# Loading, casting and transposing the first two batches in another way in a sparse attention and MLP kernel

## The chip, the cores and the metric

The kernel runs on one core of a Trainium2 chip. The metric is the device time of one execution in microseconds, the median of several runs. A core has the engines PE (TensorE: matmuls and transposes), DVE (VectorE), ACT (ScalarE), POOL (GpSimd) and SP (SyncE, which here only issues transfers). They run side by side, each in its own fixed order, and wait for one another through semaphores. Transfers run on 16 DMA engines. In this kernel SP and ACT issue theirs to one kind of queue (hardware_dynamic in the profile) and POOL to another (software_dynamic), and only transfers that POOL issues change the type on the way.

## What is computed

```python
B, H, S, D = 8, 8, 576, 64            # batches, heads, tokens, head size; 8 global tokens
scores = q @ k^T / sqrt(D)            # per batch and head
mask = (|i - j| <= 32) | is_global[i] | is_global[j]
attn = softmax(where(mask, scores, -1e9))
x = (attn @ v) laid out as [B * S, H * D]            # 4608 x 512
h = x @ w_in                                         # 512 x 2048
out = (relu(h) ** 2) @ w_out                         # 2048 x 512
```

All inputs come as fp32, the token indices as int64, and the output is fp32. Inside, the kernel works in fp16 with fp32 accumulation.

## The kernel before

**Unit of work.** Attention is done for one pair of heads of one batch at a time: pair i is heads 2(i mod 4) and the next one of batch i // 4, so i = 0 to 3 is batch 0 and i = 4 to 7 is batch 1. A pair has two halves of the query columns. For each half, `sc_mm` makes the scores in PSUM, `sc_exp` takes the exponential on ACT, `pv_mm` multiplies by the values and by a block of ones (for the row sums), `pv_rec` makes reciprocals on ACT with a logarithm and an exponential, and `pv_mul` on DVE writes the result into `xT` (or `xA`, for half 0 of batch 0).

**Masking.** It is done in one of two ways. Where `added(i, half)` is true, PE first adds a large negative number to the masked places, with a matmul of an identity and the tile `far` ahead of the scores. Elsewhere `sc_mask` on DVE multiplies the exponentials (tile `er`) by 0 or 1 (into tile `et`).

**Keys and queries.** Batches 0 and 1 are loaded as token rows by `fetch_tokens`, 96 partitions of 6 tokens for each head. Pairs 0 and 1 come as fp32 into `stf`. Pairs 2 and 3 (into `s16a`, a part of `mix`) and 4 to 7 (into `s16b`) come through POOL's queue, and turn to fp16 on the way. `cast_tokens` then copies each pair to a tile `natk` or `natq`, with the two heads side by side; for the fp16 rows this copy only changes the layout. `transpose` puts these tiles through PE, six token groups at a time, and adds a product with a one-hot matrix that picks the global tokens. `place_k` and `place_q` copy the result to `kt` and `qt`. A switch, `wide`, decides whether a weight of 128 columns is used whole or in two halves of 64; it is off in batch 0 and on in batch 1.

**Values.** `fetch_values` brings a pair's values into the fp32 tile `stv` (a part of `early`) from SP's queue, one DMA for each of 5 tiles of 120 tokens. `cast_values` makes the fp16 tile `vts[i]` from it. In batch 0 this runs on DVE (pairs 0 and 3), POOL (pair 1) and ACT (pair 2). `values_sum` and `values_place` then gather the global tokens' values and put them in rows 0 to 7 of each tile.

**Batches 2 to 7** take another way: fp16 copies in DRAM (`kscr`, `qscr`), transposed by DMA (`fetch_transposed`, SP), and values cast by DMA.

**Global query tokens.** Their columns are set afterwards by `scatter` on POOL, a copy for each token to a column whose number stands in a POOL register. `load_columns` reads those eight registers.

**The MLP** is cut into parts (`mm1`, `mm1_half`, `mm2`, `mm2_fast`) that stand in a list, `fills`. `fill` and `take` put them between the attention steps. `w_in` and `w_out` come through POOL's queue in four DMAs each.

**Order.** Nothing is scheduled automatically: each engine runs its instructions in the order of the program's text. The order of batch 0 is written out by hand (L888 to L1016), batch 1 has a loop (L1032 to L1055). `keep_warm` and `warm` are matmuls without use that fill waiting time on PE. Before SP brings batch 1's values, a small DMA named `gate` (L1012) reads a piece of `w_in`, so SP stands there until that piece has landed.

Of the kernel before, what the change touches and what calls it, by code (L numbers as in the profile page):

```python
# [17 lines left out]
KT = 120  # L18
NT = 5
KN = (120, 120, 120, 120, 96)  # L20
# [30 lines left out]
def kernel(  # L51
# [57 lines left out]

    def token_rows(nm, i):  # L110
        x = "kq".index(nm)
        if i < 2:
            one = stf[0:TP, x, 2 * FW * i : 2 * FW * (i + 1)]
        elif i < NHP:
            one = s16a[0:TP, x, 2 * FW * (i - 2) : 2 * FW * (i - 1)]
        else:
            one = s16b[0:TP, x, 2 * FW * (i - NHP) : 2 * FW * (i - NHP + 1)]
        return one.rearrange("p (h f) -> p h f", h=2)

# [29 lines left out]

    def fetch_tokens(eng, nm, i):  # L150
        b, hp = divmod(i, NHP)
        eng.dma_start(
            out=token_rows(nm, i),
            in_=src[nm][b, 2 * hp : 2 * hp + 2].rearrange("h (p j) d -> p h (j d)", j=TJ),
        )

    def fetch_values(eng, b, hp):
        hs = slice(2 * hp, 2 * hp + 2)
        for t in range(NT):
            r0 = 0 if t and not b else 8  # L160
            eng.dma_start(
                out=stv[r0 : 8 + KN[t], t, hs],
                in_=v[b, hs, KT * t + r0 - 8 : KT * t + KN[t]].rearrange("h s d -> s h d"),
            )

    kscr, qscr = {}, {}
# [52 lines left out]
    fetch_values(nc.sync, 0, 1)  # L219
    for hp in range(2, NHP):  # L220
        fetch_values(nc.sync, 0, hp)

# [4 lines left out]
    nc.vector.memset(onesb, 1.0)  # L227
    nc.vector.memset(stv[0:NG, 0], 0.0)
    pidx = sbt("pidx", [P, 4], I32)
# [56 lines left out]
    for i in range(2, NHP):  # L286
        fetch_tokens(nc.gpsimd, "k", i)
        fetch_tokens(nc.gpsimd, "q", i)


    wide = [False]

    def column_tiles():
        return (slice(0, P),) if wide[0] else (slice(0, D), slice(D, P))
# [190 lines left out]
    def transpose(nm, i, idles=0):  # L485

        nat = nats[(nm, i)]
        tr = pst("mm", [P, 1024], FP16)
        warm(tr.bitcast(FP32), idles)
        for j in range(TJ):  # L490
            for r in column_tiles():
                nc.tensor.transpose(
                    tr[r, TP * j : TP * j + TP], nat[:, j, r], identity[0:TP, 0:TP]
                )
        gl = tr.bitcast(FP32)[:, 384 : 384 + NG]
        for j in range(TJ):
            halves(
                gl, nat[:, j, :], ohp[0:TP, j, :], start=(j == 0), stop=(j == TJ - 1),
                skip_group_check=True,
            )  # L500
        trs[(nm, i)] = tr[:, 0:S].rearrange("p (j q) -> p q j", j=TJ), gl
# [250 lines left out]
    def added(i, half):  # L752
        return i < NHP and (half == 0 or i < 2) or NHP <= i < 2 * NHP and half == 0

# [134 lines left out]
    keep_warm(4)  # L889
    load_columns()  # L890
    index_base()
# [26 lines left out]
    mask_globals(mg, 1)  # L918
    cast_values(pool.tensor_copy, 1)
    casts0(2)  # L920
    sc_mm(1, 0, 2)
# [11 lines left out]
    pv_mul(0, 0)  # L933
    casts0(3)
    values_sum(1)
# [6 lines left out]
    place_q(3)  # L942
    cast_values(act, 2)
    pv_mm(1, 0)
    pv_mm(0, 1)
    cast_values(vec, 3)
    values_sum(2)
# [24 lines left out]
    for i in range(4):  # L972
        pool.dma_start(out=w_in[:, :, ts(i, 512)], in_=wv[:, :, ts(i, 512)])
    def tokens1(i):
        for nm in "kq":
            cast_tokens(vec, nm, i)

    def transposes1(i):
# [4 lines left out]

    for i in range(NHP, 2 * NHP - 1):
        fetch_tokens(pool, "k", i)
        fetch_tokens(pool, "q", i)
    scatter(0, slice(0, NHP - 1), xA)
# [10 lines left out]
    pv(2, 1)  # L998
    pv(3, 1)
    scatter(0, slice(NHP - 1, NHP), xA)  # L1000
    fetch_tokens(pool, "k", 2 * NHP - 1)
    fetch_tokens(pool, "q", 2 * NHP - 1)
    nc.scalar.copy(out=xT[:, :, 256:HS], in_=xA[:, :, 256:HS])
    for u in range(0, 8, 2):
        fills.pop(0)
        mm1_half(u, 0, range(NDM - 1, NDM))
    tokens1(NHP)
    for j in range(4):
        pool.dma_start(out=w_out[:, ts(j, 4), :], in_=wo[:, ts(j, 4), :])
    scatter(0)  # L1010
    gate = dram.tile([1, 8], FP16, name="gate")
    nc.sync.dma_start(out=gate, in_=w_in[0:1, 0, 3 * 512 : 3 * 512 + 8])  # L1012
    nc.sync.dma_start(
# [9 lines left out]
    transposes1(NHP)  # L1023
    tokens1(NHP + 1)
    take(2)
# [6 lines left out]
    for i in range(NHP, 2 * NHP):  # L1032
        scores(i, 0)
        fill(1)
        if prev is not None:
            pv(*prev)
        if i + 1 < 2 * NHP:
            transposes1(i + 1)
        fill(1)
        scores(i, 1)  # L1040
        pv(i, 0)
        if i + 2 < 2 * NHP:
            tokens1(i + 2)
        if i + 1 < 2 * NHP:
            values1(i + 1)
        fill(2)
        prev = (i, 1)
        if i == NHP:
            open_batch(2)
            fetch_batch_globals(2)  # L1050
        elif i == NHP + 1:
            fetch_batch(2, "k")
        elif i == NHP + 2:
            fetch_batch(2, "q")
            fetch_batch_values(2)  # L1055
# [75 lines left out]
```

## Time and profile before

| | |
|---|---|
| median of 5 runs | 327.25 us (327.0 to 327.77) |
| the profiled execution | 326.49 us |
| its span, first to last instruction | 324.7 us |
| PE busy / DVE / ACT / POOL | 310.3 / 244.7 / 202.2 / 127.8 us |
| mean granted TensorE clock | 0.992 |
| DMA packets, data | 149919, 39.32 MB |

The profile is of one execution. All its times are microseconds from the start of the span. A row of the timeline has the start, the length, the engine, the line of the kernel, the operation, output<-input, the shape and a count, and in brackets the idle time of that engine just before with what ended it. A line such as L298 is that of a helper that all matmuls of a kind share, so the names of the tiles tell them apart. PEld is PE loading weights, which goes on beside its matmuls. A busy PE is not PE at its peak, and the ends of matmuls are modelled.

### The profile page before, as it was taken

To read this page: it belongs to the slowest core of one execution; us is meant where nothing else is said; L and a number is where in the kernel's file an instruction comes from. 1 tells how busy PE (TensorE), PEld (TensorE's weight loads), DVE (VectorE), ACT (ScalarE), POOL (GpSimd) and SP (SyncE) were. 2 spreads that over 40 slices of the span, in tenths; PEclk is the share of its full clock that TensorE was granted. 3 is DMA by queue.
4 is the path that set the end of the run, shared out by engine and by line. 5 is a ranking of instruction groups with operands and counts; after the bars stand their busy time and mean duration, and the time that the engine had idled before them with its cause. 6 is when DMAs were issued, how large, how long until landed. Compare 5 with 4: busy or idle time off the path is not lost.

```text
span 324.7 us, 11457 instructions
## 1 busy us (share of the span) xinstructions
PE 310.3 (96%) x4739; PEld 234.9 (72%) x4739; DVE 244.7 (75%) x601; ACT 202.2 (62%) x380; POOL 127.8 (39%) x222
## 2 busy tenths in 40 slices
PE   7887899999999999999999999999999999999995
PEld 4655677445588758975999856985698569868995
DVE  6774599558997788678867869876987698768465
ACT  3684687536856685768547487658765876373150
POOL 8558697348801950289001970059302000100000
PEclk9998999999999999999999999999999999999999
DMA  8999999989995999599923699559996301200211
GB/s 193 181 193 206 191 193 167 152 108 203 138 116 77 193 163 99 77 187 142 135 94 87 53 176 152 73 108 189 136 99 129 97 0 35 100 1 2 85 48 67
DMA packets 149919, 39.32 MB, mean 121 GB/s; under 512 B 133124, under 2 KB 149300, under 8 KB 149868
## 3 DMA queue, kind: packets, MB, share of 16 engines
q0 software_dynamic: 95408, 16.78, 65.6%
q1 hardware_dynamic: 54042, 21.23, 34.8%
q8 instruction: 37, 0.61, 0.8%
q10 hardware_dynamic: 418, 0.59, 0.7%
q14 instruction: 14, 0.11, 0.1%
HBM read 37.86 MB, written 17.29 MB: 170 GB/s over the span
## 4 chain that ended last, share of the span: by engine, by line
issue 45%; POOL 22%; PE 12%; DMA 9%; POOLq 1%; ACT 1%; DVE 0%
PE mm L298 12%; DMA qscr<-in_q_dram 6%; POOL kscr L178 6%; POOL xT L873 5%; POOL s16b L207 3%; DMA kscr<-in_k_dram 3%; POOL qscr L185 3%; POOL stf L207 1%; POOL gstq L435 1%; POOL gstk L435 1%; POOL gstv L435 1%; POOLq L873 1%; ACT rec L822 0%; ACT rec L821 0%; ACT rl L543 0%
## 5 line engine op out<-in xcount | busy, mean ns | idle before, releaser
L298 PE MATMUL mm<-xT,w_in 128*64 128x512 f16 (+2 forms) x1216 | 122.5, 351 | 0.2 <-POOL xT L873 0.2
L298 PEld LDWEIGHTS <-w_in 128*64 128x64 f16 (+1 forms) x1280 | 80.1, 109 | 45.6 <-issue 3.4
L543 ACT ACTIVATE rl<-mm 128x512 f16<-128x512 f32 x128 | 75.0, 598 | 36.1 <-PE mm L298 34.3
L545 DVE TENSOR_TENSOR gt<-rl 128x512 f16<-128x512 f16 x128 | 53.0, 423 | 23.0 <-ACT rl L543 21.9
L298 PEld LDWEIGHTS <-mix 128*64 128x64 f16 x1280 | 68.8, 110 | 1.7
L873 POOL COPY xT<-gx 128x4 f16 x64 | 18.0, 282 | 130.5 <-DVE xT L852 127.1
L779 ACT ACTIVATE er<-at 128x880 f16<-128x880 f32 x54 | 46.1, 904 | 14.5 <-PE at L770 13.0
L630 DVE TENSOR_TENSOR mix<-gt 128x1024 f16<-128x1024 f16 (+1 forms) x82 | 52.9, 673 | 0.2
L789 DVE TENSOR_TENSOR et<-er,mask 128x880 f16<-128x880 f16 x54 | 33.2, 617 | 16.8 <-ACT er L779 16.2
L298 PE MATMUL mm<-early,mix 128*64 128x256 f16 x768 | 45.4, 273 | 0.0
L821 ACT ACTIVATE rec<-at 128x288 f32<-128x288 f32 x64 | 25.8, 404 | 27.1 <-PE at L811 21.9
L298 PEld LDWEIGHTS <-gt 128*64 128x64 f16 (+1 forms) x596 | 33.1, 109 | 9.8 <-DVE gt L545 2.2
L852 DVE TENSOR_TENSOR xT<-at,rec 128x288 f16<-128x288 f32 x60 | 27.2, 454 | 9.3 <-ACT rec L822 8.9
L298 PE MATMUL mm<-early,gt 128*64 128x256 f16 x512 | 32.2, 274 | 1.0 <-DVE gt L545 1.0
L298 PE MATMUL mm<-w_out,mix 128*64 128x256 f16 x512 | 30.9, 273 | 0.0
L811 PE MATMUL at<-et,onesb 128*64 128x192 f16 (+5 forms) x400 | 29.8, 225 | 0.0
L822 ACT ACTIVATE rec<-rec 128x288 f32<-128x288 f32 x64 | 28.4, 443 | 2.0
L665 DVE TENSOR_TENSOR ot<-mm,pt 128x512 f32<-128x512 f32 (+1 forms) x36 | 22.7, 632 | 6.5 <-ACT pt L690 5.2
L178 POOL DMA_DIRECT2D kscr<-in_k_dram x30 | 26.6, 1076 | 1.2 <-DMA w_out<-in_moe_w_out_dram 0.9
L185 POOL DMA_DIRECT2D qscr<-in_q_dram x24 | 23.8, 1397 | 0.5 <-DMA gscr_k<-gstk 0.5
L690 ACT COPY pt<-mm 128x512 f32<-128x512 f32 (+1 forms) x18 | 9.7, 540 | 20.6 <-PE mm L298 20.6
L811 PEld LDWEIGHTS <-onesb 128*64 128x64 f16 x400 | 21.8, 110 | 0.7
(119 smaller groups left out, 327.3 us busy)
## 6 DMA issues: line engine op xcount, KB each, us to landing
out_dram<-ot SPq DMA_DIRECT2D x32, 256.0 KB
qscr<-in_q_dram POOLq DMA_DIRECT2D x24, 144.0 KB, 8.9
kscr<-in_k_dram POOLq DMA_DIRECT2D x24, 120.0 KB, 6.0
w_in<-in_moe_w_in_dram POOLq DMA_DIRECT2D x4, 512.0 KB, 9.2
w_out<-in_moe_w_out_dram POOLq DMA_DIRECT2D x4, 512.0 KB, 12.1
stf<-in_v_dram POOLq DMA_DIRECT2D x12, 120.0 KB, 10.3
s16b<-in_v_dram POOLq DMA_DIRECT2D x12, 120.0 KB, 8.2
early<-in_v_dram SPq DMA_DIRECT2D x20, 60.0 KB
```

The source lines that it names most:

```text
L178: nc.gpsimd.dma_start(out=kscr[b][r0 : r0 + KN[t]].rearrange("s (h d) -> s h d", d=D), in_=k[b, :, KT * t : KT * t + KN[t]].rearrange("h s ...
L185: nc.gpsimd.dma_start(out=qscr[b][r0 : r0 + GTOK].rearrange("s (h d) -> s h d", d=D), in_=q[b, :, GTOK * g : GTOK * (g + 1)].rearrange("h ...
L298: nc.tensor.matmul(to[r], weights[:, r], moving, **flags)
L543: nc.scalar.activation(out=rl, in_=ph, func=AF.Relu)
L545: nc.vector.tensor_tensor(out=gt[:, :, 0:T], in0=rl, in1=rl, op=ALU.mult)
L630: nc.vector.tensor_tensor(out=gsums[p][:, lo:hi, 0:TH], in0=g[0], in1=g[1], op=op)
L779: nc.scalar.activation(out=er[:, :, 0:W], in_=scs.pop((i, half))[:, :, 0:W], func=AF.Exp, bias=0.0, scale=scale)
L789: nc.vector.tensor_tensor(out=et[:, :, 0:W], in0=er[:, :, 0:W], in1=mask[:, MB[half] : MB[half] + W].unsqueeze(1).to_broadcast((P, 2, W)), ...
L811: nc.tensor.matmul(acc[D * e : D * e + D, x, o : o + w], onesb if x else vt[:, t, e], et[:, e, so : so + w], start=(n == 0), stop=(n == le ...
L822: nc.scalar.activation(out=rec, in_=rec, func=AF.Exp, scale=-1.0)
L852: nc.vector.tensor_tensor(out=(xT if x0 else xA)[:, hp, x0 : x0 + HS].rearrange("p (k x) -> p k x", k=2), in0=av[:, 0, :, 0:GTOK], in1=rec ...
L873: nc.gpsimd.tensor_copy(out=xb[:, :, ds(gv[g], 1)], in_=gxs[b][:, pairs, g : g + 1])
```

## The change

The change has these parts:

- Values of pairs 0 and 1 still come as fp32 by SP, in three DMAs a pair instead of five. Those of pairs 2 and 3 are loaded by POOL straight into `vts[2]` and `vts[3]`, cast on the way, behind the token rows of pairs 2 and 3 and ahead of the gather and of `w_in`. Their casts on ACT and DVE are gone. Pair 1's cast moves from POOL to DVE.
- No value DMA writes rows 0 to 7 in batch 0 any more, so these are cleared first, on DVE.
- Token rows that are already fp16 (pairs 2 to 7) are transposed from where the DMA put them. `cast_tokens` is used for pairs 0 and 1 alone, and transposes and one-hot products always work in two halves of 64.
- Batch 1's pairs 5 to 7 come with one DMA for k and one for q.
- `load_columns` stands behind batch 1's loads instead of at the program's start.
- Two of the four `w_out` DMAs go ahead of the last pair's `scatter`; the gate reads chunk 2 of `w_in` instead of chunk 3.
- `added` is no longer true for half 0 of batch 1, so these scores are masked on DVE.

```diff
-    def token_rows(nm, i):
+    def token_rows(nm, i, n=1):
...
-            one = s16b[0:TP, x, 2 * FW * (i - NHP) : 2 * FW * (i - NHP + 1)]
-        return one.rearrange("p (h f) -> p h f", h=2)
+            one = s16b[0:TP, x, 2 * FW * (i - NHP) : 2 * FW * (i - NHP + n)]
+        return one.rearrange("p (h f) -> p h f", f=FW)
...
-    def fetch_values(eng, b, hp):
+    def fetch_values(eng, b, hp, to=None):
         hs = slice(2 * hp, 2 * hp + 2)
-        for t in range(NT):
-            r0 = 0 if t and not b else 8
+        to = stv[:, :, hs] if to is None else to
+        n = NT - 1
+        for h in range(2):
             eng.dma_start(
-                out=stv[r0 : 8 + KN[t], t, hs],
-                in_=v[b, hs, KT * t + r0 - 8 : KT * t + KN[t]].rearrange("h s d -> s h d"),
+                out=to[8 : 8 + KT, 0:n, h],
+                in_=v[b, 2 * hp + h, 0 : KT * n].rearrange("(t s) d -> s t d", s=KT),
             )
+        eng.dma_start(
+            out=to[8 : 8 + KN[n], n],
+            in_=v[b, hs, KT * n : S].rearrange("h s d -> s h d"),
+        )
...
-    for hp in range(2, NHP):
-        fetch_values(nc.sync, 0, hp)
...
-    nc.vector.memset(stv[0:NG, 0], 0.0)
+    nc.vector.memset(stv[0:NG, :, 0 : 2 * 2], 0.0)
+    for vt in vts[2:NHP]:
+        nc.vector.memset(vt[0:NG], 0.0)
...
     for i in range(2, NHP):
         fetch_tokens(nc.gpsimd, "k", i)
         fetch_tokens(nc.gpsimd, "q", i)
+    for i in range(2, NHP):
+        fetch_values(nc.gpsimd, 0, i, vts[i])
...
     def transpose(nm, i, idles=0):
-        nat = nats[(nm, i)]
+        if i < 2:
+            nat = nats[(nm, i)].rearrange("p j (h d) -> p j h d", d=D)
+        else:
+            nat = token_rows(nm, i).rearrange("p h (j d) -> p j h d", d=D)
...
-            for r in column_tiles():
+            for h, r in enumerate((slice(0, D), slice(D, P))):
                 nc.tensor.transpose(
-                    tr[r, TP * j : TP * j + TP], nat[:, j, r], identity[0:TP, 0:TP]
+                    tr[r, TP * j : TP * j + TP], nat[:, j, h], identity[0:TP, 0:TP]
                 )
...
-            halves(
-                gl, nat[:, j, :], ohp[0:TP, j, :], start=(j == 0), stop=(j == TJ - 1),
-                skip_group_check=True,
-            )
+            for h, r in enumerate((slice(0, D), slice(D, P))):
+                nc.tensor.matmul(
+                    gl[r], nat[:, j, h], ohp[0:TP, j, :], start=(j == 0), stop=(j == TJ - 1),
+                    skip_group_check=True,
+                )
...
     def added(i, half):
-        return i < NHP and (half == 0 or i < 2) or NHP <= i < 2 * NHP and half == 0
+        return i < NHP and (half == 0 or i < 2)
...
     keep_warm(4)
-    load_columns()
     index_base()
...
-    cast_values(pool.tensor_copy, 1)
-    casts0(2)
+    cast_values(vec, 1)
...
-    casts0(3)
...
-    cast_values(act, 2)
...
-    cast_values(vec, 3)
...
-    for i in range(NHP, 2 * NHP - 1):
-        fetch_tokens(pool, "k", i)
-        fetch_tokens(pool, "q", i)
+    for nm in "kq":
+        fetch_tokens(pool, nm, NHP)
+    for nm in "kq":
+        fetch_tokens(pool, nm, NHP + 1, NHP - 1)
+    load_columns()
     scatter(0, slice(0, NHP - 1), xA)
...
     pv(3, 1)
+    for j in range(2):
+        pool.dma_start(out=w_out[:, ts(j, 4), :], in_=wo[:, ts(j, 4), :])
     scatter(0, slice(NHP - 1, NHP), xA)
-    fetch_tokens(pool, "k", 2 * NHP - 1)
-    fetch_tokens(pool, "q", 2 * NHP - 1)
...
-    tokens1(NHP)
-    for j in range(4):
+    for j in range(2, 4):
         pool.dma_start(out=w_out[:, ts(j, 4), :], in_=wo[:, ts(j, 4), :])
...
-    nc.sync.dma_start(out=gate, in_=w_in[0:1, 0, 3 * 512 : 3 * 512 + 8])
+    nc.sync.dma_start(out=gate, in_=w_in[0:1, 0, 2 * 512 : 2 * 512 + 8])
...
-    tokens1(NHP + 1)
...
-        if i + 2 < 2 * NHP:
-            tokens1(i + 2)
```

More of the change, by code (lines that the diff above doesn't have):

```diff
@@ L148, with fetch_tokens @@
     gscr = {}
-    def fetch_tokens(eng, nm, i):
+    def fetch_tokens(eng, nm, i, n=1):
         b, hp = divmod(i, NHP)
         eng.dma_start(
-            out=token_rows(nm, i),
-            in_=src[nm][b, 2 * hp : 2 * hp + 2].rearrange("h (p j) d -> p h (j d)", j=TJ),
+            out=token_rows(nm, i, n),
+            in_=src[nm][b, 2 * hp : 2 * (hp + n)].rearrange("h (p j) d -> p h (j d)", j=TJ),
         )
-    def fetch_values(eng, b, hp):
+    def fetch_values(eng, b, hp, to=None):
         hs = slice(2 * hp, 2 * hp + 2)
-        for t in range(NT):
-            r0 = 0 if t and not b else 8
+        to = stv[:, :, hs] if to is None else to
+        n = NT - 1
+        for h in range(2):
             eng.dma_start(
-                out=stv[r0 : 8 + KN[t], t, hs],
-                in_=v[b, hs, KT * t + r0 - 8 : KT * t + KN[t]].rearrange("h s d -> s h d"),
-            )
+                out=to[8 : 8 + KT, 0:n, h],
+                in_=v[b, 2 * hp + h, 0 : KT * n].rearrange("(t s) d -> s t d", s=KT),
+            )
+        eng.dma_start(
+            out=to[8 : 8 + KN[n], n],
+            in_=v[b, hs, KT * n : S].rearrange("h s d -> s h d"),
+        )
     kscr, qscr = {}, {}
@@ L973 @@
         pool.dma_start(out=w_in[:, :, ts(i, 512)], in_=wv[:, :, ts(i, 512)])
-    def tokens1(i):
-        for nm in "kq":
-            cast_tokens(vec, nm, i)
     def transposes1(i):
```

## The prediction

> **What bounds the kernel now.** I read the page first, then busy time by stretch, then the timeline of the first 65 us engine by engine, then the DMA view of single stretches.
>
> The page and the busy time by stretch (columns: stretch, its length, then busy us and count for PE, PEld, DVE, ACT, POOL; granted TensorE clock, DMA share, GB/s):
> ```profile
> PE 310.3 (96%) x4739; PEld 234.9 (72%) x4739; DVE 244.7 (75%) x601; ACT 202.2 (62%) x380; POOL 127.8 (39%) x222
> ...
> 20.00:30.00 10.00, 6.24 (x107) 4.24 (x107) 6.37 (x21) 7.53 (x16) 5.04 (x19) 0.98 1.26 204
> 30.00:40.00 10.00, 8.59 (x95) 6.66 (x94) 4.36 (x11) 4.83 (x11) 7.27 (x15) 0.85 1.26 197
> 40.00:50.00 10.00, 10.00 (x140) 7.80 (x138) 8.77 (x29) 8.07 (x16) 8.45 (x9) 1.00 1.32 194
> ```
> From 40 us on PE is full: what takes PE work away there is worth its own time, and what only relieves DVE or POOL is worth nothing. Before about 39 us PE waits in chains with the other engines, and there one late step moves everything behind it, to the end. So I ask two things: how far does the start of the w_in product (28.96) move, and how much PE work between 36 and 65 us goes or comes.
>
> DVE in the opening (start, length, engine and line, what):
> ```profile
> 0.93 0.27 DVE L224 MEMSET idle<- 128x256 uint32 x1 [0.93 <-PEq L1115]
> ...
> 1.46 0.48 DVE L228 MEMSET early<- 8x512 f32 x1
> ...
> 2.03 0.19 DVE L309 MEMSET oh<- 128x160 uint32 x1
> ...
> 5.45 0.20 DVE L328 TENSOR_TENSOR ohp<-gbf,tokp 128x48 f16<-128x48 f32 x1
> 5.57 0.55 DVE L455 CAST natk<-stf 96x768 f16<-96x768 f32 x1
> 7.33 0.66 DVE L506 COPY kt<-mm 128x480 f16<-128x480 f16 x1 [1.21 <-PE mm L298]
> ```
> DVE runs without a gap from 0.93 to the cast of the first k rows; those landed at 3.8 by the trace's landing records. PE transposes them at once. DVE is therefore the opening's critical engine.
>
> DVE late in batch 0, and below it PE from there into batch 1:
> ```profile
> 22.09 0.23 DVE L463 CAST early<-early 104x128 f16<-104x128 f32 x1 [1.40 <-DMA early<-in_v_dram]
> 22.23 0.47 DVE L478 COPY early<-gvs 8x640 f16<-8x640 f16 x1
> ```
> ```profile
> 23.92 0.56 PE L298 MATMUL at<-far,identity 128*64 128x440 f16 x4 [0.49 <-DVE mix L852]
> ...
> 28.96 4.45 PE L298 MATMUL mm<-mix,w_in 128*128 128x256 f16 x24 [1.49 <-ACT er L779]
> ...
> 38.59 0.43 PE L492 MATMUL mm<-identity,natk 96*128 96x96 f16 x6 [0.29 <-DVE natk L455]
> ...
> 41.16 0.54 PE L298 MATMUL at<-far,identity 128*128 128x440 f16 x2
> ...
> 41.63 0.36 PE L770 MATMUL at<-qt,kt 64*128 64x160 f16 x6
> ```
> On DVE, the engine stands 1.40 us for the last tile of pair 3's values, with pairs 2 and 3's placing queued behind it. That tile left SP at 15.1 and landed at 22.1, beside w_in packets.
>
> **The change part by part.**
>
> *Opening memsets.* L228 grows from 512 to 1280 f32 elements per row. 512 took 0.44 to the next start, 0.86 ns each, so 1280 take 1.10: +0.66. Two memsets of 640 fp16 are added. If written as 320 words, like idle (256 words, 0.24 to the next start), 0.29 each; if as fp16 elements, at the 0.12 us per 128 of the ones memset (1.17 to 1.29), 0.6 each. I take the words, as idle, oh and kt are fp16 tiles that the trace shows as uint32: +0.58. Together +1.2, at most +1.9. Nothing covers it: the mask copies, one_hots, natk at 5.57, PE's transposes at 6.17 and place_k at 7.33 follow on DVE or wait for it. ACT's q cast (6.26 to 7.09) has its own start, but q's transposes stand behind k's on PE. From 13.86 to 19.75 PE is unbroken by its own order, fillers included, so the delay is carried to there: **+1.2**.
>
> *Casts out of batch 0.* On DVE pairs 2 and 3's token casts go (0.34+0.34, 0.56+0.34), pair 1's value cast comes over from POOL (0.98 there, 0.55 on DVE as for pair 0). The token casts lie before or beside that unbroken PE stretch: nothing gained; if PE were not full there, at most 0.7. Pair 1's value cast waits for its values. They were in at 13.3 with SP held back for free slots; now SP issues six DMAs at once, and DVE comes to the cast at about 14: no wait, and 0.5 us of slack before place_k(2).
>
> *Later values.* ACT's cast (0.82 at 19.26) and DVE's (with its wait) go. Without the opening's shift: values_sum(2) starts at 19.75 instead of 19.93 and runs through in 0.4; scores(3,0) end at 21.1, not 21.48; exp 21.15 to 22.08; pv_mm(2,0) at 22.2, not 22.75, ending 22.9. On DVE placing of pair 2 is at 20.6, of pair 3 at 21.6 to 22.35, pv_mul(1,0) ends at 22.75, so PE's scores(1,1) start at 22.9, not 23.92, and end at 23.75. ACT has the reciprocals of (2,0) done at 23.83, so its exp starts at 23.85 instead of 24.82: **-0.95**. The rest up to 28.96 hangs on that exp. ACT's own order stops a larger gain.
>
> *POOL's queue.* Six value DMAs (0.64 to 0.76 each by its token and weight rows: 4.2 us) go ahead of the gather and w_in. The eight index loads go behind; each held the sequencer some 0.58 (0.29 load, 0.15 register operations and gaps), 5.9 to 10.9. The gather comes at 12.6 instead of 11.65, w_in at 13.7 instead of 14.28. Batch 1's loads shrink from eight DMAs to four, and POOL's waits of 1.81 and 2.24 on w_in slots go. The index loads then run from about 18 to 23, before the scatter, which waits for DVE until about 25: hidden; without that cover up to 4.7. The two w_out DMAs now ahead of pair 3's scatter (1.5 us) end it at about 31.5, needed at 34.2: hidden.
>
> [...] In the stretch 56 to 60 us:
> ```profile
> q0 software_dynamic: 4438, 0.56, 219.8%
> ```
> packets of 128 B pass at 4438 in 4 us. [...]
>
> *Batch 1.* The diff also takes i = 4 to 7 out of `added` for half 0. PE loses two far matmuls per pair. From 41.16 to the scores at 41.63 is 0.47; the gap ahead is 0.11; without them the gap to scores is 0.20 (as at 44.59, half 1). So 0.38 each, four times: **-1.5**. DVE gains four mask products (0.62 each, 2.5) and loses eight token casts (3.1): no new bound; the product is done long before pv needs it (exp ends 42.93, pv 44.88). The wait of 0.29 at 38.59 goes: **-0.29**. Transposes now are 12+12 narrow instructions instead of 6+6 wide: 0.45 a call (9.80 to 10.27 to 10.7) against 0.415 (38.59 to 39.01 to 39.42), eight calls: **+0.3**. Merged loads land later than single ones, but q5 to q7 by about 37, used at 42.
>
> Sum: 1.2 - 0.95 - 1.5 - 0.29 + 0.3 = -1.25. The profiled execution took 326.49 (span 324.7, and 1.8 around it that the change does not touch); it would take 325.2. The median of the runs is 0.76 above it, so 327.25 becomes **326.0**.
>
> *The clock.* PE in four successive stretches:
> ```profile
> 19.50:22.92 3.42, 2.31 (x38) 1.00 1.25 205
> 22.92:26.33 3.41, 2.52 (x64) 1.00 1.24 207
> 26.33:29.74 3.41, 1.46 (x20) 0.99 1.28 201
> 29.74:33.15 3.41, 3.41 (x19) 0.51 1.32 206
> ```
> After a stretch 43% busy the clock was halved for 3.4 us; after 68% and 74% it was not. The 24 matmuls took 4.45, at the rate of 36.40 (16 in 1.91) they take 2.87: 1.6 lost. [...] My start moves +0.25, so the sum keeps the half rate; 1.6 stays for a rival. [...]
>
> **The rivals.**
>
> *Hidden anyway.* PE starts batch 2's scores at 69.62, and qt of pair 8 landed at 69.2 by the landing records. If that chain (q rows to scratch, SP's DMA transpose) does not move, PE gains 0.4 of 1.25 and waits for the rest: 326.9. Against it: DMA engines were half idle from 13.75 to 17 (some 1.6 us), which the earlier weights fill, and SP, busy with batch 1's values until 50.8, gets free sooner.
>
> *Slower.* The same landing later. The gate opens at w_in chunk 2, so 4608 value packets mix with w_in's last chunk, tokens and w_out. If that puts w_out and the gathers queued behind it from 49.4 to 51.5, qt lands at about 71.3; PE comes at 68.3, waits 3.0, and the kernel takes 327.25 + 1.75 = 329. It costs from a landing after 68.3, and is slower by over 0.2% from 70.2; halfway it is 328. For it: a margin of only 0.4. Against: total bytes are the same, and more of them start early.
>
> *Clock, either way.* The half-rate stretch is escaped: 324.4. [...]
>
> *Not as it says.* Values or tokens were late already and merged loads are later still: PE would wait at transposes; 0 to +1.
>
> **How the numbers follow.** A measurement here tells 0.2% (0.65 us) from no change. Forecast 0.45 (its own range 325.2 to 326.8, nearly all faster by more); half-rate escaped 0.13; hidden anyway 0.20; late landing 0.16; late clock or late loads 0.06. Faster 0.56, same 0.21, slower 0.23. The range 324.2 to 328.3 takes in the escaped clock and half of the late landing.
>
> **What would show it.** Right: natk at about 6.8 on DVE; no DVE wait near 22; the w_in product at 29.0 to 29.4; no far matmul after 36 us; four mask products more. Wrong: natk still at 5.6; a PE wait ahead of the scores near 68; the 0.5 clock gone or longer; PE waiting at L492 for a DMA.

## Result and profile after

The changed kernel takes 325.81 us (median of 28 runs) where the kernel before took 327.57 (49 runs): a ratio of 0.9948, with a 95% interval of 0.9931 to 0.9966, or about 1.70 us less. The forecast was 1.25 us less, so 326.0. Sign and size came out right, but several steps of the sum did not. Medians here are of all executions, while ratios leave out the few that lie over 1.5% above the fastest of their kernel, so a ratio is not always the quotient of two medians.

The profiled execution of the changed kernel took 328.16 us (span 326.4) and is not a typical one: PE ran at half rate twice in it (granted clock 0.50 from 24.75 to 28.16 and from 31.57 to 34.98). It is read here for what each engine does, and a second profile of the same kernel (`a_again` below, span 325.5, no half-rate stretch) for when. In both, line numbers are some ten higher than before: the matmul helper is L305 (was L298), the transposes L502 (L492), the scores L781 (L770).

The page of the changed kernel, then DVE in the opening (timeline):
```profile
PE 310.4 (95%) x4827; PEld 235.8 (72%) x4827; DVE 245.1 (75%) x595; ACT 201.5 (62%) x378; POOL 127.5 (39%) x222
```
```profile
1.63 1.12 DVE L231 MEMSET early<- 8x1280 f32 x1 [0.21 <-issue]
2.77 0.67 DVE L233 MEMSET early<- 8x320 uint32 x2
...
6.80 0.55 DVE L462 CAST natk<-stf 96x768 f16<-96x768 f32 x1
8.72 0.66 DVE L517 COPY kt<-mm 128x480 f16<-128x480 f16 x1 [1.37 <-PE mm L508]
```
The k cast starts at 6.80, as forecast (5.57 before). The kt copy is 1.39 later than before, and the first scores 1.60 later.

PE at the end of batch 0 and into batch 1, in the first profile:
```profile
22.72 0.24 PE L478 MATMUL mm<-early,oh 128*64 128x128 f16 x1 [1.21 <-issue]
...
31.62 4.41 PE L305 MATMUL mm<-mix,w_in 128*128 128x256 f16 x24 [1.48 <-ACT er L790]
...
40.85 0.45 PE L502 MATMUL mm<-identity,s16b 96*64 96x96 f16 x12
...
43.90 0.37 PE L781 MATMUL at<-qt,kt 64*128 64x160 f16 x6
```
and the same rows in the second:
```profile
21.92 0.24 PE L478 MATMUL mm<-early,oh 128*64 128x128 f16 x1 [0.39 <-issue]
...
29.67 2.78 PE L305 MATMUL mm<-mix,w_in 128*128 128x256 f16 x24 [1.48 <-ACT er L790]
...
37.27 0.45 PE L502 MATMUL mm<-identity,s16b 96*64 96x96 f16 x12
```
DVE's wait for values near 22 is gone, and so are the far matmuls ahead of the scores and the wait for natk ahead of the transposes. New is a PE wait in the middle of `values_sum(2)` for nothing that the profile shows ("issue"). The w_in product takes 4.41 in one profile, where the granted clock was 0.50 from 31.57 to 34.98, and 2.78 in the other, which has no such stretch. Four successive stretches of the first profile (PE busy is the first number after the length, the granted clock the third from the end):
```profile
21.33:24.75 3.42, 1.64 (x26) 0.99 (x24) 1.68 (x6) 1.67 (x5) 0.00 (x0) 1.00 1.25 206
24.75:28.16 3.41, 3.34 (x50) 2.40 (x50) 2.13 (x7) 2.52 (x6) 0.45 (x3) 0.50 1.26 204
28.16:31.57 3.41, 1.26 (x28) 0.83 (x24) 2.02 (x7) 3.19 (x6) 2.90 (x10) 1.00 1.32 196
31.57:34.98 3.41, 3.36 (x16) 2.42 (x17) 0.60 (x1) 0.00 (x0) 2.92 (x9) 0.50 1.27 200
```
Two stretches of 3.41 us in which PE was busy for 48% and 37% are each followed by one at half rate. One such stretch lowers the mean clock of an execution by 0.005 (half of 3.41 us in a span of 326.4), so the mean clock that each run lists tells how many there were. Of the first 30 executions of the changed kernel, 3 show none (324.50 to 324.76 us), 21 about one (324.79 to 327.14), 6 two (327.55 to 328.62).

The legs of the batches on PE, from the start of one mark to the next, in us. The last column is the changed kernel with fillers (matmuls without use in a waiting time), `a_warm` below. It has the legs of the changed kernel in a third profile:

| leg | before | forecast | after | again | a_warm |
|---|---|---|---|---|---|
| start to first scores | 9.47 | +1.2 | 11.07 | 11.09 | 11.05 |
| to the scores of (3,1) | 17.64 | -0.95 | 18.70 | 16.73 | 16.79 |
| to the w_in product | 1.85 | 0 | 1.85 | 1.85 | 1.85 |
| to k4's transposes | 9.63 | -0.29 | 9.23 | 7.60 | 7.61 |
| to the first scores of batch 2 | 31.03 | -1.2 | 30.30 | 31.39 | 30.81 |
| to the end | 255.1 | 0 | 255.2 | 256.9 | 254.9 |

The last leg goes with the chip and not with the kernel: it is 254.9 to 255.2 in the profiles of before, after, `b_values`, `b_batch1`, `a_warm` and `c_warm`, and 256.2 to 256.9 in all eight others, which come from two chips, whatever the kernel. So each ratio below is to the kernel before on the same chip.

### The profile page after: what moved, and what is told of

Its sections match the earlier page's. It is cut to its first block, busy times and chain, and to the rows that moved or that the text cites. A ratio compares the mean times of both kernels' runs of the same rounds, so it can differ in the third digit from the quotient of the medians.

```text
span 326.4 us, 11606 instructions
## 1 busy us (share of the span) xinstructions
PE 310.4 (95%) x4827; PEld 235.8 (72%) x4827; DVE 245.1 (75%) x595; ACT 201.5 (62%) x378; POOL 127.5 (39%) x222
## 4 chain that ended last, share of the span: by engine, by line
PE 40%; issue 27%; POOL 11%; DVE 4%; DMA 4%; ACT 2%; POOLq 1%; DVEq 0%
PE mm L305 36%; POOL kscr L183 4%; POOL xT L884 3%; DMA qscr<-in_q_dram 3%; PE at L822 2%; POOL stf L212 2%; PE at L781 2%; DVE gt L556 1%; ACT er L790 1%; DMA gstv<-in_v_dram,gidx 1%; DVE mix L641 1%; POOL qscr L190 1%; POOL gstk L442 1%; DVE xT L863 1%; DVE early L635 1%
## 5 line engine op out<-in xcount | busy, mean ns | idle before, releaser
L305 PE MATMUL mm<-xT,w_in 128*64 128x512 f16 (+2 forms) x1216 | 122.5, 351 | 0.2 <-POOL xT L884 0.2
L305 PEld LDWEIGHTS <-w_in 128*64 128x64 f16 (+1 forms) x1280 | 80.1, 109 | 45.7 <-issue 3.4
L305 PEld LDWEIGHTS <-mix 128*64 128x64 f16 x1280 | 68.9, 110 | 1.6
L790 ACT ACTIVATE er<-at 128x880 f16<-128x880 f32 x58 | 49.7, 904 | 15.4 <-PE at L781 13.9
L800 DVE TENSOR_TENSOR et<-er,mask 128x880 f16<-128x880 f16 x58 | 35.7, 617 | 17.7 <-ACT er L790 17.2
L305 PE MATMUL mm<-early,mix 128*64 128x256 f16 x768 | 45.4, 273 | 0.0
L305 PEld LDWEIGHTS <-gt 128*64 128x64 f16 (+1 forms) x596 | 33.1, 109 | 9.8 <-DVE gt L556 2.2
L305 PE MATMUL mm<-early,gt 128*64 128x256 f16 x512 | 32.2, 274 | 1.0 <-DVE gt L556 1.0
L305 PE MATMUL mm<-w_out,mix 128*64 128x256 f16 x512 | 30.9, 273 | 0.0
L822 PE MATMUL at<-et,onesb 128*64 128x192 f16 (+5 forms) x400 | 30.6, 228 | 0.0
L822 PEld LDWEIGHTS <-onesb 128*64 128x64 f16 x400 | 22.5, 113 | 0.7
```

The costliest lines, as they stand in the source:

```text
L305: nc.tensor.matmul(to[r], weights[:, r], moving, **flags)
L790: nc.scalar.activation(out=er[:, :, 0:W], in_=scs.pop((i, half))[:, :, 0:W], func=AF.Exp, bias=0.0, scale=scale)
L800: nc.vector.tensor_tensor(out=et[:, :, 0:W], in0=er[:, :, 0:W], in1=mask[:, MB[half] : MB[half] + W].unsqueeze(1).to_broadcast((P, 2, W)), ...
L822: nc.tensor.matmul(acc[D * e : D * e + D, x, o : o + w], onesb if x else vt[:, t, e], et[:, e, so : so + w], start=(n == 0), stop=(n == le ...
```

## Experiments

The theory at the start was the prediction's own sum, with the clock unchanged. The rivals were that PE stands for something else anyway, and that the clock decides.

**The changed kernel again** (`a_again`, and `a_base2` on another chip), with no edit.

> The changed kernel once more, for a second profile of it and as the measure for the other runs beside it. By the sum of the prediction it takes 1.25 us less than the kernel before; the 28 runs known give 1.7 less. The first profile had two half-clock stretches (24.75 to 28.16 and 31.57 to 34.98) and a wait of 1.21 us of PE at the third matmul of values_sum(2). If these two belong to the change, this profile shows them too. If the half-clock stretches are a matter of single executions, it shows one or none, and the w_in product starts at 29.0 to 30.5 instead of 31.6.

> The changed kernel again, as the measure of the three others beside it. Expected: 0.5% less than the kernel before. In its profile PE should stand for nothing that the profile shows (issue) at the third matmul of values_sum(2), row 705 of PE's records, until 1.3 us after a packet of 16 KB on the instruction queue landed, as in the profiles so far; and, if the wait of 0.48 at the q transposes of pair 5 belongs to the kernel and not to one chip, there too.

327.76 us, a ratio of 0.9956 (0.9918 to 0.9994), and 328.22, 0.9953 (0.9922 to 0.9983). Neither profile has a half-rate stretch, and the w_in product starts at 29.67 and 29.97: the two stretches of the first profile were a matter of that execution. The issue wait at `values_sum(2)` came again, with 0.39 and 0.74. A wait of 0.48 and 0.49 in the middle of the q transposes of pair 5 was new:
```profile
42.98 0.29 PE L502 MATMUL mm<-identity,s16b 96*64 96x96 f16 x4 [0.48 <-issue]
```
It delays the next scores by 0.78 (from the scores of (4,0) to those of (4,1) it takes 4.02, and 3.24 in the first profile). All six profiles with the narrow transposes from these two chips have it, and none of the four others with them. So, like the last leg, it goes with the chip.

**The clears out of the opening** (`a_clears`).
```diff
-    nc.vector.memset(stv[0:NG, :, 0 : 2 * 2], 0.0)      # at the start
-    for vt in vts[2:NHP]:
-        nc.vector.memset(vt[0:NG], 0.0)
...
     cast_tokens(vec, "k", 0)
+    nc.vector.memset(stv[0:NG, :, 0 : 2 * 2], 0.0)
...
     cast_values(vec, 0)
+    for vt in vts[2:NHP]:
+        nc.vector.memset(vt[0:NG], 0.0)
```


> The changed kernel with its clears of rows 0 to 7 off DVE's opening: the fp32 one goes behind the cast of the first k rows, where DVE stood 1.37 us for PE, the two fp16 ones behind the cast of pair 0's values, where it stood 0.53. Theory (the clears are on the opening's critical chain): the k cast is at 5.0 instead of 6.8, the first scores at 9.5 or earlier instead of 11.07, and everything up to the w_in product comes 1.2 to 1.6 us earlier: 324.2 to 324.6 against 325.8. Rival (PE's order, the fetch of its instructions or the clock take it back before 40 us): no more than 0.3 us less than the changed kernel.

326.58 us, 1.18 less than the changed kernel beside it (ratios 0.9915, 0.9887 to 0.9944, against 0.9956; the intervals overlap). The clears were on the critical chain: in its profile the k cast starts at 5.32, 1.5 earlier, and the first scores at 8.75, 2.3 earlier (the clock is behind most of the other 0.8, see the part on the prediction). But the gain was not kept there: this profile has a half-rate stretch at 12.51 to 15.92, the third scores start at 17.65 (17.77 in `a_again`) and the w_in product at 29.72. The median says 1.2; this one profile can't show where it remains.

**Values by SP again, index loads early again** (`a_values`).
```diff
+    for hp in range(2, NHP):
+        fetch_values(nc.sync, 0, hp)
...
-    for i in range(2, NHP):
-        fetch_values(nc.gpsimd, 0, i, vts[i])
...
     keep_warm(4)
+    load_columns()
...
+    cast_values(act, 2)
     pv_mm(1, 0)
     pv_mm(0, 1)
+    cast_values(vec, 3)
...
-    load_columns()
     scatter(0, slice(0, NHP - 1), xA)
```


> The changed kernel with pairs 2 and 3's values again by SP as fp32 and cast by ACT and DVE, and with the index loads at the program's start again (the two had changed places in POOL's queue). The opening's clears stay as long as they are in the changed kernel; the further clear stands in a wait of DVE. Theory (the sum's step of -0.95): 0.9 to 1.0 us slower than the changed kernel, with the exp of (1,1) later by that. Rival (PE stands at values_sum(2) for its own instructions anyway, 1.2 us in the profile of the changed kernel): within 0.3 us of the changed kernel.

329.65 us, 1.89 more than the changed kernel beside it: more than both theories said, though the intervals overlap (ratio 0.999, 0.9956 to 1.0024, against 0.9918 to 0.9994). It did not bring the old wait back: with three DMAs a pair instead of five, pair 3's values came in time and DVE never stood for them. In its profile PE stands for instructions twice, 0.51 at 17.06 and 0.96 at 23.03, 1.08 more than in `a_again`, out of 1.82 that the leg to the scores of (3,1) is longer. So it does not measure the step of -0.95, but it led to the next question.

**What PE waits for in `values_sum(2)`.** The trace also records the packets of an instruction queue (`q8 instruction: 37, 0.61, 0.8%` in the page before). One of 16 KB ends ahead of the third matmul of `values_sum(2)`, and that matmul starts so much later:

| kernel | packet ends | matmul starts | later by | wait |
|---|---|---|---|---|
| before | 19.07 | 20.41 | 1.34 | 0.21 |
| after | 21.41 | 22.72 | 1.31 | 1.21 |
| a_again | 20.63 | 21.92 | 1.29 | 0.39 |
| a_clears | 20.64 | 21.97 | 1.33 | 0.57 |
| a_values | 21.65 | 23.03 | 1.38 | 0.96 |

The weight load of this matmul is record 705 of PE in all five (all its records counted together, from 0); `a_values` stands at record 449 as well, 256 records earlier, 1.32 after the packet before. That fits a PE that runs through what a packet brings, 256 records, and waits for the next: in the profile before, 9478 matmuls and weight loads stand against the 37 packets of q8, 256 for each. From record 449 to record 705 it took 5.1 to 6.0 us in these profiles. In `b_added` (below) it took 4.8 without a wait: its packet had ended 3.1 after record 449, against 3.8 to 4.6 here.

**Fewer instructions for the same work** (`a_wide`): the switch `wide` on from the start, so that fillers and far matmuls are not cut in halves; the transposes stay narrow.
```diff
-    wide = [False]
+    wide = [True]
```


> The changed kernel with the switch wide on from the start: the fillers and the far matmuls of batch 0 work with 128 weight columns at once, half as many instructions in the same PE time; the transposes stay narrow. Theory (PE stands at values_sum(2) for its own instructions, as 256 of them run in less than the 5.2 us that the next packet needs): the wait of 0.4 to 1.4 us there goes or falls under 0.2, and the w_in product starts that much earlier: 0.3 to 1.0 us faster than the changed kernel. Rival (the wait is for values or for a buffer): the same wait at the same matmul, no change.

327.93 us against 328.22 for the changed kernel beside it (ratios 0.9921, 0.9888 to 0.9953, and 0.9953: a gain within the uncertainty). The wait went, though the same matmul comes only 60 records earlier:
```profile
21.68 0.44 PE L478 MATMUL mm<-early,oh 128*64 128x128 f16 x5
```
All five matmuls run through, and the w_in product starts at 29.59 instead of 29.97. A wait for values or for a buffer would have stayed. The 0.49 at pair 5's q transposes did stay, at the same transposes 60 records earlier, and no packet of 16 KB ends ahead of it by 1.3 us: that is another cause, which is open.

**Masking by DVE alone** (`b_added`): the kernel before with one line changed.
```diff
-        return i < NHP and (half == 0 or i < 2) or NHP <= i < 2 * NHP and half == 0
+        return i < NHP and (half == 0 or i < 2)
```


> The kernel before with one part of the change alone: half 0 of batch 1 masked by a product on DVE instead of a far matmul on PE. Theory (PE is full from 40 us on, 8 matmuls of 0.19 us taken out of it): 1.5 us faster than the kernel before, 325.8 where that takes 327.3. Rival (DVE at 75 to 88% there becomes the bound, or pv waits for the product): 0 to 0.7 faster. Rival (hidden: PE waits for the first tiles of batch 2 near 68): 0.4 faster.

330.13 us, a ratio of 1.0004 (0.9966 to 1.0042): no gain that shows. The waits of PE in its profile, from 20 to 75 us (total, times, longest), show DVE as the bound:
```profile
PE at L811 <- DVE xT L852: 0.7, 3, 0.3
PE mm L298 <- DVE kt L513: 0.5, 1, 0.5
```
From k4's transposes to batch 2 it needs 30.84 against 31.03 before. Eight token casts and four mask products together are too much for DVE there. Up to the scores of (5,0) the far matmuls gave what was forecast or nearly so; from (5,1) on, DVE's waits took it back.

**Casts back, masking kept** (`a_nat`): the same pair of loads on DVE, reached from the changed kernel.
```diff
-        if i < 2:
+        if i < 2 or i >= NHP:
             nat = nats[(nm, i)].rearrange("p j (h d) -> p j h d", d=D)
...
+            if i >= NHP:
+                nc.tensor.transpose(
+                    tr[:, TP * j : TP * j + TP], nats[(nm, i)][:, j, :], identity[0:TP, 0:TP]
+                )
+                continue
...
+        if i + 2 < 2 * NHP:
+            tokens1(i + 2)
```


> The changed kernel with batch 1's token rows cast to natk and natq on DVE again and transposed whole (6 and 6 instead of 12 and 12); the masking on DVE stays. Theory (the narrow transposes cost PE 0.07 to 0.16 a pair, and their doubled instructions cost waits for instructions; but DVE can't do casts and mask products both, as the run of the masking alone had kt 0.5 late and three waits for xT): from k4's transposes to the first scores of batch 2 about 30.8, and the total within 0.5 us of the changed kernel. Rival (the casts cost nothing and the narrow transposes do): 29.9 for that stretch, 0.4 us or more faster than the changed kernel.

328.30 us, equal to the changed kernel beside it (328.22). The leg is 30.94, with the same kt wait of 0.50 and xT waits of 0.3 as in `b_added`, and without the 0.49 in the transposes. So casts with whole transposes and no casts with narrow ones cost about the same, as long as the narrow ones bring their waits for instructions (31.37 in `a_base2`; 30.30 in the first profile, which has none there).

**Batch 1's part alone** (`b_batch1`): masking by DVE and transposes in place, on the kernel before; `transpose` is that of the changed kernel.
```diff
-        return i < NHP and (half == 0 or i < 2) or NHP <= i < 2 * NHP and half == 0
+        return i < NHP and (half == 0 or i < 2)
...
-    casts0(2)
-    casts0(3)
-    tokens1(NHP)
-    tokens1(NHP + 1)
-        if i + 2 < 2 * NHP:
-            tokens1(i + 2)
```


> The kernel before with the PE part of the change alone: half 0 of batch 1 masked by DVE, and all fp16 token rows transposed in place in halves, so without their casts. Loads, values, clears and index loads are those of before. Theory (far matmuls -1.5, the wait for natk -0.29, narrow transposes +0.3): 1.5 us faster. What the profiles of the changed kernel showed (from k4's transposes to the first scores of batch 2 30.3 against 31.03, or 31.4 where PE stood 0.5 at the q transposes of pair 5): 0 to 1.0 faster. If that wait of 0.5 comes here too, it belongs to the transposes in place and not to the loads.

328.56 us, a ratio of 0.9999 (0.9973 to 1.0025). The profile is of the fastest of its 13 executions (325.79, without half rate). In it the first rival of the prediction came true, and the wait for instructions grew:
```profile
22.30 0.24 PE L471 MATMUL mm<-early,oh 128*64 128x128 f16 x1 [1.78 <-issue]
...
69.00 0.56 PE L774 MATMUL at<-qt,kt 64*128 64x160 f16 x12 [0.65 <-DMA qt<-qscr]
```
PE was early for batch 2 and waited for qt of pair 8, which the kernel before has at 69.2. In the changed kernel it lands at 65.6, and in `a_warm` at 67.3. The clock is a part of the rest: its mean over all 13 is 0.9887, where the kernel before has 0.9912 on this chip. It is not all, as one execution at 0.999 took 329.58; that stays open. The wait at pair 5's transposes did not come here. One of 0.17 came at pair 7's (0.32 in `a_warm`, below), 1.29 after an instruction packet ended (1.35 there), so that one is of the known kind. What the one at pair 5 is stays open.

**The values' part alone** (`b_values`), with all clears behind the opening and the index loads where the changed kernel has them.
```diff
-    for hp in range(2, NHP):
-        fetch_values(nc.sync, 0, hp)
...
+    for i in range(2, NHP):
+        fetch_values(nc.gpsimd, 0, i, vts[i])
...
-    load_columns()
...
-    cast_values(act, 2)
-    cast_values(vec, 3)
...
+    load_columns()
     scatter(0, slice(0, NHP - 1), xA)
```


> The kernel before with the values' part of the change alone: values in three DMAs a pair, those of pairs 2 and 3 by POOL straight into place ahead of the gather and w_in, no casts of them on ACT and DVE, the index loads before the scatter. All clears stand in waits of DVE behind the opening, so the 0.44 of the clear before is saved as well. Theory (the sum's step of -0.95): no wait of DVE near 22, and from the first scores to the w_in product 18.6 (19.49 before, less 0.95) in a profile with no half-clock stretch in between; 0.9 to 1.4 us faster than the kernel before. Rival (PE's wait for its own instructions at row 705 takes part of it back): 0.4 to 0.8 faster, that wait 0.4 or more.

330.32 us, a ratio of 1.0064 (1.0036 to 1.0092): slower. The step itself is right: from the first scores (8.72) to those of (3,1) (25.32) it takes 16.60, against 17.64, so 1.04 less where 0.95 was forecast. The loss is behind it, in POOL's queue and then on PE (timelines):
```profile
25.16 0.63 POOL L152 DMA_DIRECT2D s16b<-in_q_dram  x1 [3.10 <-DMA w_in<-in_moe_w_in_dram]
30.67 3.85 POOL L877 COPY mix<-gx 128x3 f16 x16 [4.88 <-issue]
```
```profile
32.72 1.65 PE L302 MATMUL mm<-mix,w_in 128*128 128x256 f16 x7 [7.04 <-DMA s16b<-in_k_dram]
```
Batch 1's tokens come in single loads here, POOL stands 3.10 for a `w_in` transfer (the releaser in its row) until 25.16, and only then reads its eight indices: 4.88 us without cover. The w_in product starts at 32.72, which is when the first eight scatter copies would be done (2.0 us after 30.67, by the length of such eight in `a_again`). The profile names a DMA as the releaser; by these times the copies are likelier. PE idles for 7 us, and the clock is then at half rate for three stretches (26.76 to 37.0).

**Clears and wide together** (`a_best`).

> The changed kernel with the clears out of DVE's opening and with wide on from the start. Theory: the two gains add, 1.2 for the clears and 0.3 to 1.0 for the instructions, 1.5 to 2.2 us faster than the changed kernel. Rival (both only move the start of batch 1 relative to the windows of the clock): no more than the clears alone, 1.2.

327.30 us, a ratio of 0.9922 (0.9894 to 0.995), 0.92 less than the changed kernel beside it (0.9953; the intervals overlap): no sum of the two. Its profile has two half-rate stretches, at 11.65 to 15.06 and 28.72 to 32.13.

**Fillers ahead of the w_in product** (`a_warm` on the changed kernel, `c_warm` on `a_best`).
```diff
     sc_mm(3, 1)
+    warm(pst("mm", [P, 512]), 5)
```


> The changed kernel with five fillers (128x512 matmuls in halves, about 0.24 us each at the full clock) between the scores of (3,1) and the w_in product, where PE waits 1.48 us for ACT's exponentials. Theory (the half-clock stretch follows a window of 3.41 us in which PE was busy half of it or less): the stretch at 28 to 35 us goes; nearly all executions show a clock over 0.997, and the median falls by 0.5 to 1.0 us against the changed kernel (to a ratio of about 0.992 to the kernel before). Rival (the half clock is not set by PE's idle time there): as many executions at 0.995 and below as with the changed kernel, no gain.

> All three together: clears out of the opening, wide from the start, and the five fillers ahead of the w_in product. Theory: a ratio of 0.988 to 0.990 to the kernel before, the fastest of all. Rival (the half-clock stretch that the kernel with clears and wide showed at 11.7 to 15.1 stays and its loss moves on): 0.991 to 0.992, as without the fillers.

`a_warm`: 324.44 us (324.16 to 324.72), where the kernel before took 328.21 on the same chip: a ratio of 0.9886 (0.9852 to 0.992), and all five executions at a mean clock of 0.998 to 1.0.
```profile
28.14 1.27 PE L305 MATMUL mm<-idle 128*64 128x512 f16 x10
29.69 2.78 PE L305 MATMUL mm<-mix,w_in 128*128 128x256 f16 x24 [0.28 <-ACT er L790]
```
The product starts no earlier than in `a_again` (29.67), and the time is that of the first executions of the changed kernel without a half-rate stretch (324.50 to 324.76). So the fillers take away the half rate and nothing else. The changed kernel without them was not run on this chip, and the kernel before was not run with them. `c_warm`: 325.25 us, 0.9931 (0.9902 to 0.996). Its profile is the shortest of all (span 322.2), but 8 of its 11 executions show one half-rate stretch and take 325.6 (their median); which one, no profile shows.

## Why the prediction was right, and where it was not

- **Opening memsets, +1.2.** As forecast on DVE (1.12 and 0.67 long, k cast +1.23), and PE starts the far matmuls ahead of the first scores 1.23 later too. But the scores came 1.60 later, as these four matmuls took longer (before, then changed):
```profile
8.80 0.74 PE L298 MATMUL at<-far,identity 128*64 128x456 f16 x4
10.03 1.10 PE L305 MATMUL at<-far,identity 128*64 128x456 f16 x4
```
  From their start to the scores it is 0.67 before and 1.03 in the changed kernel. Where the clock's first record of full rate lies ahead of them it is 0.51 (`a_clears`, `a_values`, `a_nat`). This record is at 9.17 in the profile before, in the midst of them, and at 11.09 and 11.02 in two profiles of the changed kernel. So the missing 0.4 goes with a late clock, which had a part in the prediction's chances (late clock or late loads, 0.06) and came true. `a_clears` shows that nothing covers the clears.
- **Casts out of batch 0, nothing gained.** Pair 1's cast on DVE took 1.07, not 0.55, but DVE did not wait for its values, and PE's order from the first scores to the third was as before (6.68 and 6.69 us).
- **Later values, -0.95.** 1.04 in `b_values`, 0.91 and 0.85 in the changed kernel (`a_again`, `a_warm`), where PE's wait for instructions takes part of it back (that wait was 1.21 in the first profile). The wait was in the trace of before (0.21 <-issue, in part hidden behind ACT's cast), and the sum left it out.
- **The w_in product at 29.0 to 29.4.** Missed: 29.67 and 29.97, by the late clock in the opening and the wait for instructions, and 31.62 in the first profile, with half rate ahead of it.
- **POOL's queue, index loads hidden.** Right in the changed kernel, with loads merged. `b_values` shows the price without that cover: 4.88 us, where 4.7 was named. The second `w_in` chunk landed at 23.0, where it was 24.2 before, with the values' packets of 128 B ahead of it.
- **Far matmuls, -1.5, and the wait for natk, -0.29.** Adding these two was the step that failed. Three of the four pairs gave 0.37 to 0.39 each, as worked out (scores (5,1) to (6,0): 3.03 before, 2.65 after). At pair 4 the two saved the same time. The end of DVE's placing of qt before; k4's transposes and the scores in `b_added`; that end and the scores in `a_warm`:
```profile
41.12 0.18 DVE L525 CAST qt<-mm 128x32 f16<-128x32 f32 x1
```
```profile
41.11 0.43 PE L492 MATMUL mm<-identity,natk 96*128 96x96 f16 x6 [0.29 <-DVE natk L455]
...
43.87 0.37 PE L770 MATMUL at<-qt,kt 64*128 64x160 f16 x6
```
```profile
40.11 0.18 DVE L536 CAST qt<-mm 128x32 f16<-128x32 f32 x1
...
40.35 0.37 PE L781 MATMUL at<-qt,kt 64*128 64x160 f16 x6
```
  Before, qt is in place at 41.30, 0.33 ahead of the scores, so the far matmuls hold them. Taken out alone (`b_added`), they bring the scores from 3.04 to 2.76 after k4's transposes, and then qt holds them. In the changed kernel k4's transposes start 0.36 earlier, but DVE first has a product to make that waits for ACT (0.22), so qt is hardly earlier: 2.99 after the transposes (40.29 against 37.30 in `a_warm`), and the scores at 3.05. From the w_in product ahead of k4's transposes to these scores it takes 5.23 before, 4.96 in `b_added` and 4.89 in the changed kernel: 0.34 saved where 0.67 was forecast. In the legs, the far matmuls give -1.13 instead of -1.5.
- **Narrow transposes, +0.3.** 0.06 a pair for 6 and 7, as forecast, but 0.28 for pair 5: 0.40 in all, and up to 0.8 more where PE stood in them. With it the leg from k4's transposes to batch 2 is -0.73 in the first profile, -0.22 in `a_warm`, +0.36 in `a_again`, where -1.2 was forecast.
- **No new bound on DVE.** Right for the reason given, that the casts go: with the casts kept, DVE is the bound (`b_added`, `a_nat`).
- **The clock.** The sum kept the half rate during the w_in product, and a start without it was a rival at 0.13. It decided more than that: the profiles of `a_again`, `a_base2` and `a_wide` have no such stretch. On three chips the executions of the kernel before have a mean clock of 0.9912 to 0.9920, those of the changed kernel, on two of these, 0.9936 and 0.9958: some 0.4 and 0.7 of a stretch less. A clock under 0.986, three stretches or more, is in 19 of 91 executions of the kernel before and in 1 of 54 of the changed kernel. For the comparison of the forecast itself this can't be told: there the changed kernel has 0.9927, and the clocks of the kernel before are not on record.

So the legs alone, with half rate in the w_in product on both sides, don't make the gain: 1.6 - 0.9 - 0.4, and -0.7, -0.2 or +0.4 for batch 1, is between -0.4 and +0.7. Two things stand beside them. The half rate is missing more often in the changed kernel, at 1.6 us for the w_in product; and the profile of the kernel before, from which the legs are taken, is of an execution that was 1.1 us faster than its median (326.49 against 327.57). Grouped by the half-rate stretches that the mean clock tells, the medians of the changed kernel are lower by 1.05 (none) and 0.95 (one) on one chip, and by 1.73 and 0.84 on another. So the terms were named rightly, but an overestimate in batch 1 and a cost in the opening that was missed were made up by gains that were not counted, and the total agreed: that is luck. How the 1.70 divides exactly stays open: the mean clock counts stretches at half rate without telling where they lie, or when PE first came to full rate (from 4.8 to 18.8 us in these profiles), and there is one profile of the kernel before.

Once the full rate had come, no wait of PE outside `b_values` was longer than 1.8 us, and the half rate came all the same. The prediction's row (halved after a stretch 43% busy, not after 68% and 74%) is now a range: once PE had come to full rate, a stretch of 3.41 us with PE busy for 36 to 51% of it was followed by half rate in all nine cases, one with 52 to 57% in none of five. Two in the opening, with 58 and 65% (`a_clears`, `a_best`), were followed by it all the same. In each of the 14 profiles the changes of the granted clock lie a whole number of 3.413 us apart (9.17, 29.65 and 33.07 in the profile before: six steps and one), and where this grid falls against the kernel differs from execution to execution. So the same waits of PE are shared out among the stretches in another way each time.

"Hidden anyway" and "late landing" did not happen: qt of pair 8 landed at 65.6 to 67.3 in three profiles, earlier than before and ahead of PE. The first happens when batch 1's part is done alone.

## What to carry to other kernels

A removed instruction is worth its time only where its engine is the last to arrive: look at each place for what else lands just then, as qt did at pair 4, and do not add two savings that may end at the same next wait. Look at the clock of every execution before reading a gain of half a per cent; a few fillers in a known PE wait brought about as much here (0.6 of a per cent beyond the change, by five executions on another chip) as the whole rebuilding of loads and casts. On `a_best` they brought nothing that shows (0.9931 against 0.9922). And parts of a change may only work together: the index loads are free behind merged loads, the DVE masks without the casts, and PE's gain with an early qt.

## What the hardware showed that was not expected

- PE stood 0.21 to 1.78 us in `values_sum(2)` with no releaser in the profile ("issue"), most likely for its own instructions: this wait ended 1.3 to 1.4 us after a 16 KB packet on the instruction queue ended (1.5 in `b_batch1`), and such waits were seen at records 256 apart (449 and 705 in `a_values`). PE was there in stretches of small matmuls with a weight load each (narrow transposes, half-width far matmuls). With half the instructions for the fillers and far matmuls (`a_wide`) the wait of 0.74 (`a_base2`) went.
- Half rate came for 3.41 us at a time, after a stretch of the same length in which PE was busy for 36 to 51% (58 and 65% twice in the opening), though outside `b_values` no single wait was longer than 1.8 us. It came on a grid of 3.413 us whose place differs between the profiles (full rate from 9.17 before and from 11.09 in the changed kernel, half rate from 12.51 in `a_clears` and from 11.65 in `a_best`). Fillers of 1.27 us in all made the stretch from 28.03 to 31.44 92% busy, and no half rate followed.
- The dense part from batch 2 to the end took 254.9 to 255.2 us in six profiles and 256.2 to 256.9 in eight others, taken on two chips.
